# A ConvNeXt-V2 block on one core: where rstd's broadcast stands, which quarters are channel-major, and who normalises one block in ten

## The chip, the core and the metric

The kernel runs on one core of a Trainium2 chip. The metric is the device time of one execution in microseconds, told as the median of several runs. The core's engines are TensorE (PE, with its weight loads shown as PEld), VectorE (DVE), ScalarE (ACT), GpSimd (POOL) and SyncE (SP), which here only issues DMAs.

## The reference

The input x is one image of 512 x 512 pixels with 96 channels, in bf16. E is 384.

```python
out = sum over i, j of xp[:, i:i+H, j:j+W, :] * dw[i, j]      # 3x3 depthwise convolution
h = _layernorm(out, axis=-1)                                  # over the 96 channels
h = gelu(einsum('bhwc,ce->bhwe', h, w1))                      # 96 -> 384
gx = sqrt((h * h).sum(axis=(1, 2), keepdims=True) + 1e-6)     # per channel, over the whole image
nx = gx / (gx.mean(axis=-1, keepdims=True) + 1e-6)
h = grn_gamma * (h * nx) + grn_beta + h
return x + einsum('bhwe,ec->bhwc', h, w2)                     # 384 -> 96
```

The sum of squares over the whole image stands between the two matrix products, so everything up to gelu has to be seen once before the second product can begin.

## The kernel before, in words

The image is cut into 128 blocks of four rows (`NBLK`, `GR`). The kernel has two phases. The first computes the convolution, the normalisation, the first product and gelu of every block, and gathers the sum of squares per channel. The second phase makes gelu again or takes it from where it was kept, multiplies it by the scaled w2, and adds x. The change is in the first phase alone.

The first phase is a software pipeline written out by hand, in slots. In slot s the convolution of block s runs, and the first product of a block some 14 earlier (`mlp`). A table `at`, filled by `put(slot, what, block or batch)`, says which stages belong to a slot, and the loop over s issues them in a fixed order. Every instruction is kept in program order on its engine, so this order is also the queue of each engine, SP's DMA queue included. From the middle of the first phase on, ten slots follow a fixed cycle, since the kinds of blocks repeat with the block's number modulo ten.

The stages that matter here:

- `load_x`, `turn_x`: SP loads the rows of x, and VectorE transposes them into channel-major form (tile xT).
- `conv_taps`: TensorE makes the 3x3 convolution as three bursts of 24 small matmuls (PS<-xT,Wq). `evac` copies the result to y_bf: ScalarE alone (128x1536), or, when the block of the slot's first product has exactly two channel-major quarters (`shared`), ScalarE two thirds and VectorE one third.
- `stage_sq` (GpSimd squares y_bf into ysq), `stage_stats` (TensorE sums over channels, rowsel matmuls), `stage_moments` (VectorE).
- `stage_rstd`, `stage_newton`: GpSimd's small operations that make 1/sqrt(variance) for a batch of four blocks. `stage_turn`: VectorE transposes the result (rt<-rstd). `stage_rows`: SP writes it to DRAM (r_dram<-rt, two DMAs). `stage_bcast`: SP reads it back, spread over partitions (rbc<-r_dram, four DMAs).
- `stage_norm`: GpSimd multiplies y_bf by rbc (yn<-y_bf,rbc). `stage_write` and `stage_read` take yn through DRAM to the layout of the first product (ynT).
- `mlp_units`: the first product of a block, in nine units; each is some matmuls into PSUM followed by one gelu of ScalarE into g. PSUM gives the units one buffer of two banks and two of one bank.

The sum of squares has two ways. A block's 2048 pixels are four quarters. A quarter that is channel-major (`cm_quads` says how many the block has) has its channels on partitions; VectorE reads it with three bn_stats (`entry`, bst<-g). A quarter that is pixel-major has its pixels on partitions; TensorE multiplies it with itself in 128x128 matmuls (gram matmuls, PS<-g), of which the diagonal is used. `grams` is the list of what is owed, two entries for each pixel-major quarter, and each entry is six matmuls. `gram_next(n)` runs the next n entries. In the slot of a block its own entries are added at the end, so they run in later slots. With the convolution running, each slot calls `gram_next(1)` twice.

Blocks whose number modulo ten is in `WHOLE` (0, 3, 7) have four channel-major quarters, and their g is stored to DRAM; the others have two or three. The slot's order of the stages above the product is:

```python
load_x(s + 4); stage_read; stage_write; stage_bcast; stage_rows; store_next()
stage_newton(k, pool); stage_sq; stage_norm; stage_rstd(k, pool)
```

For a batch whose last statistics are made in slot t, rstd is due in t+1, newton and turn in t+2, rows in t+3, the broadcast in t+4, and the first block's norm in t+5.

Of the kernel before, what the change touches and what calls it, by code (L numbers as in the profile page):

```python
# [17 lines left out]
BATCH = 4  # L18
NHELD = 5
WHOLE = (0, 3, 7)  # L20
NTAIL = 14
GRB = 3

# [33 lines left out]
def kernel(  # L57
# [23 lines left out]
    NBLK = H // GR  # L81
# [18 lines left out]
    def cm_quads(q):  # L100
        if is_whole(q) or is_held(q):
            return NQ
        if q > HELD[0]:
            return 1
        return 2 if q >= NBLK - 16 or (q - 1) % 10 in WHOLE else 3

    whole = [q for q in range(NBLK) if is_whole(q)]
    g_dram = dram.tile([len(whole), 128, NQ * NCH * QW], bf16, name="g_dram")
# [78 lines left out]
    with ExitStack() as p1:  # L187
        pe, dve, act, pool, sp = (InOrder(tc, e) for e in (nc.tensor, nc.vector, nc.scalar, nc.gpsimd, nc.sync))
# [324 lines left out]
        def stage_sq(b, on_act):  # L513
            q = ysqpool.tile([128, NI, W], bf16, name="ysq")
            if on_act:
                act.activation(out=q[:], in_=ybf[b][:], func=ACTF.Square)
            else:
                pool.tensor_tensor(out=q[:], in0=ybf[b][:], in1=ybf[b][:], op=ALU.mult)
            ysq[b] = q
# [88 lines left out]
        def stage_turn(k):  # L608
            NT = (BATCHES[k][1] * GR * NG + 31) // 32 * 32
            rt = rtpool.tile([128, NS], bf16, name="rt")  # L610
            dve.transpose(out=rt[:, :NT], in_=rns.pop(k)[:, :NT])
            rts[k] = rt
# [19 lines left out]
        def stage_bcast(k):  # L632
            b0, n = BATCHES[k]
            rbc = rbcpool.tile([128, BATCH, W], bf16, name="rbc")
            for j in range(GR):
                sp.dma_start(out=rbc[32 * j:32 * j + 32, :n, :].rearrange("p n w -> p (n w)"),
                             in_=bass.AP(r_dram[b0].tensor, r_dram[b0].offset + j * n * W, [[0, 32], [1, n * W]]))
            rbcs[k] = rbc
# [39 lines left out]
        def mlp_tail(b, get):  # L678
            if is_held(b) or b < HELD[0]:
                gs[b] = gpool.tile([128, NQ, NCH, QW], bf16, name="g")[:]  # L680
            elif b > NBLK - 4:
                gs[b] = late.gr.tile([128, NQ, NCH, QW], bf16, name="gr")[:]
            else:
                gs[b] = g_over
            for t in range(NQ):
                cm = t < cm_quads(b)
                (cm_unit if cm else px_unit)(gs[b], ynts[b], t)
                gram_next(1)
                if cm:
                    for j in range(NCH):  # L690
                        entry(b, j, t)
                if t == 1:
                    for k in get("turn"):
                        stage_turn(k)
                if t == 2:
                    for b2 in get("stats"):
                        stage_stats(b2)
                if t > cm_quads(b):
                    grams.extend((b, (t - 1) * QC + k * E) for k in range(0, GR, 2))
            for k in get("moments"):  # L700
                stage_moments(k)
            if cm_quads(b) < NQ:
                grams.extend((b, (NQ - 1) * QC + k * E) for k in range(0, GR, 2))
# [49 lines left out]
        def store_next():  # L753
            if stores:
                b, h = stores.pop(0)
                n = NCH * QW * NQ // 3
                sp.dma_start(out=g_dram[whole.index(b)][:, h * n:h * n + n],
                             in_=flat(b)[:, h * n:h * n + n])
# [41 lines left out]
        def put(s, what, v):  # L800
            at.setdefault((s, what), []).append(v)
# [4 lines left out]
        for k, (b0, n) in enumerate(BATCHES):  # L806
            for b in range(b0, b0 + n):
                quick = b not in mlp_slots
                put(b if quick else b + 1, "sqa" if quick else "sqp", b)
                last_s = b + 1 if quick else b + 2  # L810
                put(last_s, "stats", b)
            ramp = b0 + n <= RAMP
            if ramp:
                put(last_s, "chain", k)
                put(last_s + 1, "spread", k)
            else:
                put(last_s, "moments", k)
                put(last_s + 1, "rstd", k)
                put(last_s + 2, "newton", k)
                put(last_s + 2, "turn", k)  # L820
                put(last_s + 3, "rows", k)
                put(last_s + 4, "bcast", k)
            for b in range(b0, b0 + n):
                last_norm = s = max(last_norm + 1, last_s + (1 if ramp else 5))
                put(s, "norma" if ramp else "norm", b)
                put(s + 1, "write", b)
                put(s + 2, "read", b)
                m = s + (3 if ramp else 4)
                mlp_slots.add(m)
                put(m, "mlp", b)  # L830
                put(m + is_whole(b), "combine", b)
                last_slot = m
# [4 lines left out]
        turn_x(2)  # L837
        for s in range(last_slot + 1):
            get = lambda kind: at.get((s, kind), [])
            if s + 4 < NBLK:  # L840
                load_x(s + 4)
            for b in get("read"):
                stage_read(b)
            for b in get("write"):
                stage_write(b)
            for k in get("bcast"):
                stage_bcast(k)
            for k in get("rows"):
                stage_rows(k)
            store_next()  # L850
            for k in get("newton"):
                stage_newton(k, pool)
            for b in get("sqp"):
                stage_sq(b, False)
            for b in get("norm"):
                stage_norm(b)
            for k in get("rstd"):
                stage_rstd(k, pool)
            mlp = get("mlp")

            def spread_out():
                for k in get("spread"):
# [6 lines left out]
            if mlp and mlp[0] >= TAIL0:  # L869
                assert not taps  # L870
                square_owed()
                mlp_tail(mlp[0], get)
            elif not mlp:
                if s + 3 < NBLK:
                    turn_x(s + 3)
                for f in taps:
                    f()
                if not spare:
                    spread_out()
                if evac:  # L880
                    evac()
                for b in get("sqa"):
                    stage_sq(b, True)
                for b in get("stats"):
                    stage_stats(b)
                for k in get("moments"):
                    stage_moments(k)
                if spare:
                    spread_out()
                for k in get("chain"):  # L890
                    stage_moments(k)
                    stage_chain(k)
                for k in get("turn"):
                    stage_turn(k)
                gram_next(2)
                square_owed()
            else:
                b = mlp[0]
                unit, squares, squares_rest = mlp_units(b)
                conv = lambda n, fence=True: taps[n](fence) if taps else None  # L900

                conv(0)
                unit(0, 2)
                unit(2, 1)
                squares(0)
                conv(1, False)
                spread_out()
                if s + 3 < NBLK:
                    turn_x(s + 3)
                unit(3, 1)  # L910
                unit(4, 2)
                squares(1)
                gram_next(1 if taps else 2)
                shared = evac is not None and cm_quads(b) == 2
                unit(6, 1)
                if not shared:
                    squares(2)
                unit(7, 1)
                for k in get("turn"):
                    stage_turn(k)  # L920
                conv(2)
                if evac:
                    evac(shared)
                if shared:
                    squares(2)
                gram_next(1 if taps else 2)
                unit(8, 2)
                unit(10, 1)
                for b2 in get("stats"):
                    stage_stats(b2)  # L930
                unit(11, 1)
                for k in get("moments"):
                    stage_moments(k)
                squares_rest(2)
                square_owed()
                if is_whole(b):
                    owed.append(lambda f=squares_rest: f(3))
                grams.extend((b, c) for c in range(cm_quads(b) * QC, NQ * QC, 2 * E))
                if is_whole(b):
                    stores.extend((b, h) for h in range(3))  # L940
# [130 lines left out]
```

## Time and profile before

| what | value |
|---|---|
| median of 3 runs | 1479.4 us (1470.68 to 1481.37) |
| span of the profiled execution | 1475.6 us; its time with what lies around the span isn't listed |
| PE busy | 1394.1 us, 94% |
| VectorE busy | 1183.4 us, 80% |
| ScalarE busy | 1405.9 us, 95% |
| GpSimd busy | 1300.9 us, 88% |
| bn_stats of g (bst<-g) | 1110 of 672 ns, 673.0 us busy |
| norm on GpSimd (yn<-y_bf,rbc) | 126 of 3111 ns |
| gram matmuls (PS<-g, 128x128) | 1464 |
| DMA | 422.03 MB, mean 286 GB/s |

Busy times are shares of the whole span. The first phase ends near 950 us. A wait is written as engine, tile, line, then what ended it, then microseconds in total, count and longest. In a timeline the columns are start, length, engine, line, operation, output<-inputs, shapes, count, and in brackets the idle time of the engine just before it and what ended that. L35 is the line of the helper that records every instruction, so rows are told apart by their tiles.

### The profile page before, as it was taken

How to read it: one execution, taken by the hardware profiler on the slowest of the kernel's cores; microseconds unless marked ns; L12 is line 12 of the kernel's file. 1: busy time of each engine (PE TensorE's matmuls, PEld its weight loads, DVE VectorE, ACT ScalarE, POOL GpSimd, SP SyncE). 2: the span in 40 equal slices, each digit the busy share in tenths (PEclk: the TensorE clock that was granted, in tenths of full speed). 3: DMA queues.
4: the chain of work that ended last, by engine and by line, in shares of the span. 5: the costliest groups of instructions: out<-in, count | busy, mean ns of one | idle time of the engine just before them, and what ended most of it. 6: DMA issues, size and time to landing. Idle time of an engine off the chain costs nothing.

```text
span 1475.6 us, 54538 instructions
## 1 busy us (share of the span) xinstructions
PE 1394.1 (94%) x23125; PEld 810.0 (55%) x23125; DVE 1183.4 (80%) x2174; ACT 1405.9 (95%) x1595; POOL 1300.9 (88%) x923
## 2 busy tenths in 40 slices
PE   8889899999899999999999998889999999999998
PEld 3434444444444444444444445457777777777776
DVE  8849989999899999999999997965555555555555
ACT  7889999999899999999998999999999999999997
POOL 3469989998899999999999998379999999999998
PEclk9999999999999999999999999999999999999999
DMA  6677778888788888888898876669999999999998
GB/s 180 197 204 231 245 231 275 249 266 240 244 254 268 262 275 239 271 258 272 249 276 247 267 230 200 177 226 366 358 328 383 402 392 392 405 381 406 389 390 315
DMA packets 167913, 422.03 MB, mean 286 GB/s; under 512 B 34326, under 2 KB 84182, under 8 KB 163190
## 3 DMA queue, kind: packets, MB, share of 16 engines
q1 hardware_dynamic: 151428, 314.98, 66.0%
q0 software_dynamic: 14880, 103.43, 18.6%
q8 instruction: 181, 2.97, 0.8%
q14 instruction: 62, 0.51, 0.1%
q10 hardware_dynamic: 1362, 0.15, 0.1%
HBM read 262.16 MB, written 156.22 MB: 284 GB/s over the span
## 4 chain that ended last, share of the span: by engine, by line
POOL 31%; PE 22%; ACT 13%; DVE 12%; DMA 11%; issue 7%; SPq 3%; POOLq 0%; ACTq 0%; DVEq 0%
PE PS L35 22%; POOL xb L328 17%; ACT g L35 8%; DVE bst L35 8%; POOL yn L35 7%; DMA xin<-in_x_dram 3%; ACT y_bf L35 3%; SPq L35 3%; DMA ynT<-yn_dram 3%; POOL xr L283 2%; DMA rbc<-r_dram 2%; DVE xT L35 2%; DMA yn_dram<-yn 2%; POOL ysq L35 1%; POOL var L35 1%
## 5 line engine op out<-in xcount | busy, mean ns | idle before, releaser
L35 ACT ACTIVATE g<-PS 128x512 bf16<-128x512 f32 (+2 forms) x1062 | 730.7, 842 | 26.0 <-PE PS L35 22.4
L35 DVE BATCH_NORM_STATS2 bst<-g 128x6 f32<-128x512 bf16 x1110 | 673.0, 672 | 23.5 <-ACT g L35 23.4
L35 ACT ACTIVATE gr<-PS 128x1536 bf16<-128x1536 f32 x360 | 498.5, 1457 | 14.8 <-PE PS L35 10.0
L35 POOL TENSOR_TENSOR yn<-y_bf,rbc 128x1536 bf16<-128x1536 bf16 x126 | 391.6, 3111 | 84.1 <-DMA rbc<-r_dram 50.5
L35 DVE TENSOR_TENSOR o_sb<-PS,xb 128x384 bf16<-128x384 f32 x512 | 277.7, 556 | 221.3 <-PE PS L35 172.0
L35 PE MATMUL PS<-xT,Wq 64*32 64x511 bf16 (+1 forms) x9198 | 347.6, 388 | 29.2 <-DVE y_bf L35 11.7
L328 POOL TENSOR_TENSOR xb<-xr,B2c 128x1536 f32<-128x1536 bf16 x118 | 368.4, 3136 | 1.5
L35 PE MATMUL PS<-ynT,w1p 128*128 128x512 bf16 x1161 | 332.7, 383 | 24.0 <-ACT g L35 5.8
L35 POOL TENSOR_TENSOR ysq<-y_bf 128x1536 bf16<-128x1536 bf16 x114 | 314.1, 2756 | 11.0 <-ACT y_bf L35 9.6
L35 PE MATMUL PS<-ynT,w1s 128*128 128x512 bf16 x1020 | 275.5, 379 | 0.0
L35 PEld LDWEIGHTS <-gr 128*128 128x128 bf16 x4296 | 212.1, 98 | 61.0 <-issue 3.0
L35 PE MATMUL PS<-W2s,gr 128*128 128x96 bf16 x4224 | 223.4, 206 | 2.0 <-DVE o_sb L35 1.8
L35 PEld LDWEIGHTS <-Wq 64*32 64x32 bf16 x9216 | 111.4, 90 | 201.4 <-issue 159.0
L35 ACT ACTIVATE y_bf<-PS 128x1536 bf16<-128x1536 f32 (+2 forms) x135 | 181.7, 1351 | 15.7 <-PE PS L35 10.6
L35 DVE STREAM_TRANSPOSE xT<-xin 128x576 f32<-128x576 f32 (+1 forms) x256 | 181.4, 748 | 12.8 <-DMA xin<-in_x_dram 10.6
L35 PEld LDWEIGHTS <-w1p 128*128 128x128 bf16 x1161 | 89.8, 98 | 180.3 <-issue 123.3
L35 PEld LDWEIGHTS <-g 128*128 128x128 bf16 (+1 forms) x1707 | 105.5, 98 | 89.1 <-issue 57.0
L35 PE MATMUL PS<-w1p,ynT 128*128 128x256 bf16 (+2 forms) x822 | 125.0, 272 | 8.0 <-ACT xT L35 3.2
L35 PE MATMUL PS<-g 128*128 128x128 bf16 x1464 | 123.1, 221 | 4.1 <-DVE PS L35 4.1
L35 PEld LDWEIGHTS <-w1s 128*128 128x128 bf16 x1020 | 81.9, 98 | 40.5
L35 PEld LDWEIGHTS <-gl 128*128 128x128 bf16 x1680 | 83.1, 98 | 30.0 <-issue 8.9
L35 PE MATMUL PS<-W2s,gl 128*128 128x96 bf16 x1680 | 90.3, 206 | 5.2 <-DVE o_sb L35 4.6
(109 smaller groups left out, 708.4 us busy)
## 6 DMA issues: line engine op xcount, KB each, us to landing
xin<-in_x_dram SPq DMA_DIRECT2D x126, 432.0 KB
g_dram<-g SPq DMA_DIRECT2D x105, 512.0 KB
gl<-g_dram POOLq DMA_DIRECT2D x35, 1536.0 KB, 10.7
yn_dram<-yn SPq DMA_DIRECT2D x512, 96.0 KB
ynT<-yn_dram SPq DMA_DIRECT2D x128, 384.0 KB
out_dram<-o_sb SPq DMA_DIRECT2D x127, 384.0 KB
xr<-in_x_dram POOLq DMA_DIRECT2D x123, 384.0 KB, 6.6
ynT<-yn_dram SPq DMA_DIRECT2D x255, 128.0 KB
```

Of the source, the lines that this page charges most:

```text
L35: r = f(*a, **k)
L283: pq.dma_start(out=xr[:], in_=x[0, r0:r0 + GR].rearrange("r w c -> (r w) c").rearrange("(p g) c -> p g c", g=PXP))
L328: pq.tensor_tensor(out=xb[:], in0=grp[q]["xr"][:], in1=bias[:, None, :].to_broadcast([128, PXP, C]), op=ALU.add)
```

## The change

It has three parts, all in the first phase.

1. The turn of a batch moves from slot t+2 to t+3 and to the head of the slot, in every kind of slot. The broadcast (still in t+4) moves to the head too, ahead of the x load, the read and the write; the rows move behind the g store.
2. `TWOS` replaces the old rule for two channel-major quarters: blocks 1, 4, 5, 8 and 9 modulo ten have two (before: 1, 4 and 8), and only 2 and 6 have three. In a slot with a convolution, all gram entries owed are run in that slot, half of them at the first call and the rest at the second.
3. In a slot whose product is that of a block 5 modulo ten (`DNORM`), the norm due there is done by VectorE, after the product's fifth unit, and not by GpSimd.

```diff
+TWOS = (1, 4, 5, 8, 9)
+DNORM = 5
...
-        return 2 if q >= NBLK - 16 or (q - 1) % 10 in WHOLE else 3
+        return 2 if q >= NBLK - 16 or q % 10 in TWOS else 3
...
-                put(last_s + 2, "turn", k)
+                put(last_s + 3, "turn", k)
...
             get = lambda kind: at.get((s, kind), [])
+            for k in get("turn"):
+                stage_turn(k)
+            for k in get("bcast"):
+                stage_bcast(k)
             if s + 4 < NBLK:
                 load_x(s + 4)
             for b in get("read"):
                 stage_read(b)
             for b in get("write"):
                 stage_write(b)
-            for k in get("bcast"):
-                stage_bcast(k)
+            store_next()
             for k in get("rows"):
                 stage_rows(k)
-            store_next()
...
+            mlp = get("mlp")
             for b in get("norm"):
-                stage_norm(b)
+                if not (s < NBLK and mlp and mlp[0] % 10 == DNORM):
+                    stage_norm(b)
...
                 unit(4, 2)
+                if b % 10 == DNORM and taps:
+                    for b2 in get("norm"):
+                        stage_norm(b2, dve)
                 squares(1)
-                gram_next(1 if taps else 2)
+                gram_next((len(grams) + 1) // 2)
...
                 unit(7, 1)
-                for k in get("turn"):
-                    stage_turn(k)
                 conv(2)
...
-                gram_next(1 if taps else 2)
+                gram_next(len(grams))
```

The two other calls of `stage_turn` (in slots without a product and in the last blocks' routine) go as well.

More of the change, by code (lines that the diff above doesn't have):

```diff
@@ L691, in mlp_tail @@
                         entry(b, j, t)
-                if t == 1:
-                    for k in get("turn"):
-                        stage_turn(k)
                 if t == 2:
@@ L854 @@
                 stage_sq(b, False)
+            mlp = get("mlp")
             for b in get("norm"):
-                stage_norm(b)
+                if not (s < NBLK and mlp and mlp[0] % 10 == DNORM):
+                    stage_norm(b)
             for k in get("rstd"):
                 stage_rstd(k, pool)
-            mlp = get("mlp")
             def spread_out():
@@ L892 @@
                     stage_chain(k)
-                for k in get("turn"):
-                    stage_turn(k)
                 gram_next(2)
@@ L918 @@
                 unit(7, 1)
-                for k in get("turn"):
-                    stage_turn(k)
                 conv(2)
```

## The prediction

> **What bounds the kernel now.** I read the page's busy table first, then windows over the first phase, then the waits, then two short timelines. The table shows four compute engines nearly full:
>
> ```profile
> PE 1394.1 (94%) x23125; PEld 810.0 (55%) x23125; DVE 1183.4 (80%) x2174; ACT 1405.9 (95%) x1595; POOL 1300.9 (88%) x923
> ```
>
> The average hides the phases. The change touches only the first phase (convolution and first matrix product, up to about 950 us). So I cut its regular part into nine stretches of ten slots, one slot for each block's first matrix product (blocks 20 to 109):
>
> ```profile
> core 0: us, PE busy (x) PEld busy (x) DVE busy (x) ACT busy (x) POOL busy (x), PEclk, DMA share, GB/s
> 216.64:286.32 69.68, 67.61 (x1231) 33.12 (x1230) 69.48 (x124) 69.32 (x101) 62.82 (x55) 1.00 0.86 272
> 286.32:357.90 71.58, 68.37 (x1231) 33.39 (x1230) 69.85 (x125) 69.60 (x101) 66.57 (x45) 1.00 0.79 240
> 357.90:433.51 75.61, 69.29 (x1231) 33.66 (x1230) 71.08 (x127) 69.88 (x101) 66.74 (x55) 0.98 0.84 258
> ...
> sum 645.76, PE 617.54 PEld 300.55 DVE 632.38 ACT 627.39 POOL 599.27; mean PE 68.62 PEld 33.39 DVE 70.26 ACT 69.71 POOL 66.59
> ```
>
> The columns after the length are busy microseconds. Ten slots take 71.75 us on average (645.76 / 9). VectorE is busy 70.26 of them, ScalarE 69.71, GpSimd 66.59. The best ten took 69.68 us, with VectorE and ScalarE both full; the worst took 75.61. So there is a floor near 69.7 that VectorE and ScalarE set together, and 71.75 - 69.68 = 2.07 us per ten slots in which somebody waits. The waits of the span and one long stall say who:
>
> ```profile
> POOL yn L35 <- DMA rbc<-r_dram: 50.5, 17, 12.0
> DVE rt L35 <- POOL rstd L35: 17.4, 9, 4.5
> PE PS L35 <- DVE y_bf L35: 11.7, 13, 4.3
> ```
>
> ```profile
> 368.03 3.11 POOL L35 TENSOR_TENSOR yn<-y_bf,rbc 128x1536 bf16<-128x1536 bf16 x1 [3.23 <-DMA xin<-in_x_dram]
> ...
> 375.69 0.25 DVE L35 STREAM_TRANSPOSE rt<-rstd 128x64 bf16<-128x64 bf16 x1 [2.93 <-POOL rstd L35]
> 376.56 1.28 PE L35 MATMUL PS<-xT,Wq 64*32 64x512 bf16 x23 [4.30 <-DVE y_bf L35]
> 378.42 0.60 ACT L35 ACTIVATE g<-PS 128x512 bf16<-128x512 f32 x1 [5.10 <-PE PS L35]
> ```
>
> This is one chain: GpSimd starts its normalisation 3.23 us late (it waited for the broadcast rstd; the releaser named is the queue's neighbour), so its Newton steps are late, so VectorE stands 2.93 us in front of the turn of rstd. Queued behind the turn is VectorE's third of the evacuation (y_bf), so TensorE stands 4.30 us and ScalarE 5.10. GpSimd can't catch up: two long operations a slot plus the rstd chain every fourth slot leave it little.
>
> TensorE's own pace shows in a slot whose block has two channel-major quarters:
>
> ```profile
> 391.97 0.88 PE L35 MATMUL PS<-xT,Wq 64*32 64x512 bf16 x24
> ...
> 393.45 0.50 PE L35 MATMUL PS<-g 128*128 128x128 bf16 x6
> 393.79 0.60 PE L35 MATMUL PS<-w1p,ynT 128*128 128x384 bf16 x4
> ...
> 395.13 0.51 PE L35 MATMUL PS<-g 128*128 128x128 bf16 x6
> 395.47 0.82 PE L35 MATMUL PS<-w1p,ynT 128*128 128x128 bf16 x6
> 396.13 0.45 PE L35 MATMUL PS<-rowsel,y_bf 128*128 128x4 bf16 x12
> ...
> 398.78 0.86 PE L35 MATMUL PS<-xT,Wq 64*32 64x512 bf16 x24
> ```
>
> Starts count here, since ends overlap. From one convolution to the next, 391.97 to 398.78, is 6.81 us with almost no gap: TensorE runs at about 6.8 us a slot. Six gram matmuls (PS<-g) take 0.34 us (393.45 to 393.79), and every slot has two such sets.
>
> **The change, part by part.** By the program's order it has 66 fewer bn_stats of g, 22 more VectorE casts of y_bf, 264 more gram matmuls, and 11 normalisations on VectorE instead of GpSimd. Per ten slots that is two more blocks with two quarters and one VectorE normalisation.
>
> VectorE: 6 bn_stats go, at 0.60 us from start to start (seven in 4.23 us in the row at 376.43): -3.6. Two casts come, at 0.58 (375.85 to 376.43): +1.2. One normalisation comes; its only VectorE rows are the ramp's two, 0.938 us each: +0.9. Sum -1.5, so 70.26 becomes 68.8.
>
> ScalarE: twice the evacuation shrinks from 128x1536 to 128x1024. From start to start that is 1.34 against 0.90 us (388.65 to 389.99; 395.60 to 396.50): -0.9, so 68.8.
>
> GpSimd: one normalisation of 3.11 us less: 66.59 becomes 63.5. It gets room to recover after a late transfer.
>
> TensorE: four more gram sets at 0.34 us: +1.4. The third quarter itself costs the same either way: six pixel-major matmuls take 0.66 us (395.47 to 396.13), three 128x512 at 0.22 take 0.65.
>
> That +1.4 is unevenly spread. Before, two sets ran in each slot. Now everything owed by the block before runs at once: none after a whole block, two sets after one with three quarters, four after one with two, half of them in the middle and half after the convolution. Slots 0 to 9 of a ten get 4, 0, 4, 2, 0, 4, 4, 2, 0, 4 sets. I take a slot as the larger of TensorE's and ScalarE's need, because the product has only a two-bank and two one-bank buffers between them:
> - no set (1, 4, 8): TensorE 6.81 - 0.68 = 6.13; ScalarE 6.98 (a three-quarter slot, 405.71 to 412.69) - 0.44 = 6.54. Takes 6.55.
> - two sets (3, 7, both whole blocks): as now, 7.03.
> - four sets (0, 2, 5, 6, 9): 6.81 + 0.68 = 7.49. Slots 2, 5 and 9 follow a slot with none, in which TensorE can run about 0.15 ahead (an estimate from when the buffers come free): 7.33. For 0 and 6 I take 7.45.
>
> Sum: 3 x 6.55 + 2 x 7.03 + 3 x 7.33 + 2 x 7.45 = 70.6 us per ten slots. It lies above VectorE's 68.8 and GpSimd's 63.5, so both have slack and I let the waits of 2.07 go: 71.75 - 70.6 = 1.15 us gained per ten slots. The bounds: 68.8 per ten if buffers smooth the bursts wholly; 71.9 if light slots stay at the 6.83 that two-quarter slots take now and each heavy one costs 7.4 to 7.6.
>
> The turn: it leaves the middle of one slot for the head of the next, some 3 us later, and so waits less for Newton. Queued behind it on VectorE are the slot's bn_stats and the cast. Late next would be the rows' DMAs: they were issued at 414.39, the turn was at 406.21, so 8 us of cover become 5. Price 0; without that cover, up to 3 us a batch.
>
> The broadcast: it now stands directly behind the rows on SP (before, 5.7 us apart: 414.39 and 420.05), so SP waits for the rows to land. No row shows that landing. It is at least the 0.6 us of an issue and at most the 4.86 us of a 96 KB yn_dram transfer in the chain of waits; I take 2. Behind it stand an x load (four slots ahead), a ynT read (two slots ahead of its use), four yn writes (three buffers) and a g store. SP's issues in four slots come to about 20 of 28 us, so 0 is charged; if that slack were gone, 3 us per batch. The broadcast itself lands 2 to 3 us sooner. rstd's own operations are the same.
>
> VectorE's normalisation can't meet a late broadcast: it takes blocks 9, 19, 29 and so on, never the first of a batch of four.
>
> In all, blocks 5 to 113 make 10.9 tens: 10.9 x 1.15 = 12.5 us. The second phase isn't touched. The profiled span is 1475.6 us (what lies around it isn't listed); the median is 1479.4, the runs 1470.68 to 1481.37, so the span is an ordinary one. 1475.6 - 12.5 = 1463.1; on the median, 1467.
>
> **Rivals.**
> *The bursts are absorbed.* VectorE and ScalarE at 68.8, with small waits, give at best the 69.68 already seen or a little less: 2.1 to 2.9 us per ten, 23 to 32 in all, so 1447 to 1456. For it: PEld's column is only 47% of the stretch. Against it: two-quarter slots already run at TensorE's pace of 6.81, with no gap to fill.
> [...]
>
> *Nothing moves.* The waits are fed by transfers that stay late (the read and write of yn through DRAM), and the bursts eat what the lighter VectorE gives: 1479.
>
> *Slower: TensorE becomes the bound in half the slots.* Light slots stay at 6.83 and heavy ones cost 7.4 to 7.6, so ten slots take 71.9 without any wait; with 1.2 us of the present 2.07 still lost they take 73.1: 10.9 x 1.4 = 15 us more, 1494. It decides once what is won in the light slots and on waits is under 1.3 us per ten. For it: five of ten slots are above 7 us by TensorE alone. Against it: ScalarE's 0.44 us are real in every light slot.
>
> *The turn waits all the same.* If GpSimd stays late by a slot, the turn at the slot's head stands where it stood. VectorE stood 7.7 us in front of it between 200 and 880 us, some 0.8 per ten slots, which leaves 0.35 of the 1.15: 4 us, 1475.
>
> **How the numbers follow.** Forecast 0.50 (own range 1457 to 1477), absorbed 0.20, nothing moves or the turn still waits 0.15, slower 0.15. A measurement tells about 1% from no change, 14.8 us: 1464.6 and 1494.2. Faster: all of the absorbed case and 0.18 of the forecast, 0.38. Slower: some 0.12, from the slower case, whose middle lies at that bound and whose upper part reaches 1505. Same: 0.50. The range 1448 to 1492 leaves out the best end of the absorbed case and the upper half of the slower one.
>
> **What would show it.** Right: ten-slot stretches of 70 to 71 us, with no DVE wait for rstd and no POOL wait for rbc over 1 us; slots with four sets 7.3 to 7.5 us, those with none 6.5 to 6.6; ScalarE idle in the heavy slots behind PE PS. Wrong: heavy slots at 7.0 (absorbed), light ones at 6.8 (slower), or stalls of 3 us and more that stay; a VectorE wait for rbc; SP's loads of x late.

## The result, and the profile after

The changed kernel takes 1486.82 us (median of 16 runs, 1477.79 to 1493.42) against 1477.5 for the kernel before (16 runs beside them, 1470.68 to 1484.99). The ratio is 1.0056, 95% interval [1.0037, 1.0074]: some 8 us slower, where the forecast was 12.5 faster. The profiled execution took 1479.93 (span 1478.1); it is one of the fastest of its kernel, so its trace holds less of the loss than an ordinary run. That matters below.

The busy row of the page after:

```profile
PE 1407.7 (95%) x23455; PEld 827.9 (56%) x23455; DVE 1170.4 (79%) x2137; ACT 1398.9 (95%) x1595; POOL 1266.4 (86%) x912
```

VectorE, ScalarE and GpSimd have less to do than before, TensorE more, as planned, and the time still rises. The nine stretches of ten slots (blocks 20 to 109), in the columns that were used for the kernel before (two of them and the sum):

```profile
...
434.75:505.74 70.99, 69.15 (x1261) 34.81 (x1260) 69.09 (x122) 68.93 (x101) 63.42 (x45) 1.00 0.83 253
505.74:579.49 73.75, 70.29 (x1261) 35.11 (x1260) 67.44 (x120) 69.49 (x101) 63.50 (x55) 1.00 0.80 248
...
sum 643.79, PE 625.64 PEld 313.99 DVE 621.19 ACT 622.06 POOL 573.70; mean PE 69.52 PEld 34.89 DVE 69.02 ACT 69.12 POOL 63.74
```

No stretch is under 70.99, and the mean is 643.79 / 9 = 71.53. VectorE at 69.02, ScalarE at 69.12 and GpSimd at 63.74 all have slack on average; three of the nine stretches take 71.0, with nothing late in them. That is TensorE's bursts. A slot with four gram sets, by TensorE's timeline:

```profile
256.08 0.87 PE L37 MATMUL PS<-xT,Wq 64*32 64x512 bf16 x24
256.88 0.86 PE L37 MATMUL PS<-ynT,w1p 128*128 128x512 bf16 x3
257.58 0.83 PE L37 MATMUL PS<-g 128*128 128x128 bf16 x12
...
259.59 0.84 PE L37 MATMUL PS<-g 128*128 128x128 bf16 x12
260.27 0.82 PE L37 MATMUL PS<-w1p,ynT 128*128 128x128 bf16 x6
...
263.57 1.16 PE L37 MATMUL PS<-xT,Wq 64*32 64x512 bf16 x24
```

Each pair of sets now stands together (x12, 0.67 and 0.68 us to the next start), and from convolution to convolution it is 263.57 - 256.08 = 7.49 us.

The waits inside the stretches (216 to 865 us), first in the kernel before:

```profile
POOL yn L35 <- DMA rbc<-r_dram: 13.6, 11, 2.1
PE PS L35 <- DVE y_bf L35: 10.3, 10, 4.3
DVE rt L35 <- POOL rstd L35: 7.7, 5, 2.9
```

and in the changed one:

```profile
DVE xT L37 <- DMA xin<-in_x_dram: 4.9, 3, 2.1
PE PS L37 <- DVE y_bf L37: 1.8, 4, 0.7
POOL yn L37 <- DMA rbc<-r_dram: 1.6, 1, 1.6
```

GpSimd's wait for rbc has fallen, TensorE's for y_bf too, and VectorE's for rstd is gone. What has grown is VectorE's wait in front of the turn of x (2.2 us in two stands before): its loads land late. The two long stands of the three are what made the worst stretch, 505.74 to 579.49. For the first of them, in SyncE's queue:

```profile
526.28 1.84 SPq L37 DMA_DIRECT2D r_dram<-rt  x2
530.54 2.11 SPq L37 DMA_DIRECT2D rbc<-r_dram  x4
532.70 0.42 SPq L37 DMA_DIRECT2D xin<-in_x_dram  x1
```

and on VectorE and TensorE a few microseconds on:

```profile
538.60 1.44 DVE L37 STREAM_TRANSPOSE xT<-xin 128x576 f32<-128x576 f32 x2 [2.01 <-DMA xin<-in_x_dram]
...
541.13 0.67 DVE L37 CAST y_bf<-PS 128x512 bf16<-128x512 f32 x1
...
541.85 0.86 PE L37 MATMUL PS<-xT,Wq 64*32 64x512 bf16 x23 [0.63 <-DVE y_bf L37]
```

SyncE holds the broadcast until the rows have landed (rows issued at 526.28, broadcast at 530.54), then issues its four DMAs, and only then the x load, at 532.70. VectorE wants that load in the next slot, stands 2.01 us, and gets it at 538.6, 5.9 us after its issue. Behind the turn its share of the evacuation is late, and TensorE waits for it. In all of the stretches SyncE's queue waited for the rows (total, count, longest):

```profile
SPq L37 <- DMA r_dram<-rt: 33.0, 22, 2.4
```

### The profile page after: what moved, and what is told of

Its sections match the earlier page's. It is cut to its first block, busy times and chain, and to the rows that moved or that the text cites. A ratio compares the mean times of both kernels' runs of the same rounds, so it can differ in the third digit from the quotient of the medians.

```text
span 1478.1 us, 55169 instructions
## 1 busy us (share of the span) xinstructions
PE 1407.7 (95%) x23455; PEld 827.9 (56%) x23455; DVE 1170.4 (79%) x2137; ACT 1398.9 (95%) x1595; POOL 1266.4 (86%) x912
## 4 chain that ended last, share of the span: by engine, by line
PE 27%; POOL 26%; ACT 18%; DMA 10%; DVE 9%; issue 5%; SPq 4%; ACTq 0%; POOLq 0%; DVEq 0%
PE PS L37 27%; POOL xb L330 21%; ACT g L37 13%; DMA yn_dram<-yn 7%; DVE bst L37 5%; SPq L37 4%; ACT y_bf L37 3%; POOL xr L285 3%; DVE xT L37 2%; DMA r_dram<-rt 1%; ACT xT L37 1%; ACT gr L37 1%; DMA xin<-in_x_dram 1%; POOL yn L37 1%; POOL gl L296 1%
## 5 line engine op out<-in xcount | busy, mean ns | idle before, releaser
L37 DVE BATCH_NORM_STATS2 bst<-g 128x6 f32<-128x512 bf16 x1044 | 639.3, 674 | 49.9 <-ACT g L37 49.2
L37 POOL TENSOR_TENSOR yn<-y_bf,rbc 128x1536 bf16<-128x1536 bf16 x115 | 356.8, 3105 | 52.4 <-ACT rbc L37 25.2
L37 PE MATMUL PS<-xT,Wq 64*32 64x511 bf16 (+1 forms) x9198 | 342.2, 388 | 15.5 <-ACT y_bf L37 4.1
L37 PE MATMUL PS<-ynT,w1p 128*128 128x512 bf16 x1095 | 310.4, 382 | 26.8 <-ACT g L37 5.6
L37 PEld LDWEIGHTS <-w1p 128*128 128x128 bf16 x1095 | 84.2, 97 | 183.0 <-issue 119.1
L37 ACT ACTIVATE y_bf<-PS 128x1024 bf16<-128x1024 f32 (+2 forms) x135 | 169.4, 1260 | 16.2 <-PE PS L37 10.6
L37 PE MATMUL PS<-w1p,ynT 128*128 128x384 bf16 (+1 forms) x954 | 148.8, 273 | 12.0 <-ACT xT L37 3.2
L37 PEld LDWEIGHTS <-g 128*128 128x128 bf16 (+1 forms) x1971 | 117.3, 98 | 64.1 <-issue 39.1
L37 PEld LDWEIGHTS <-ynT 128*128 128x128 bf16 x954 | 74.6, 97 | 62.2 <-issue 39.2
```

Source lines behind the costliest of these rows:

```text
L37: r = f(*a, **k)
```

## The experiments

Each ratio is to the kernel before, run on the same chip beside it (its medians there lay between 1472.3 and 1477.5), so ratios are compared and not medians. "Order", "quarters" and "norm" are parts 1, 2 and 3 of the change.

| run | order | quarters | norm on VectorE | further edit | median us | ratio, 95% |
|---|---|---|---|---|---|---|
| changed kernel | yes | yes | yes | | 1486.82 | 1.0056 [1.0037, 1.0074] |
| p1_order | yes | | | | 1473.38 | 1.0009 [0.9992, 1.0026] |
| p2_quarters | | yes | | | 1481.12 | 1.0067 [1.0043, 1.0092] |
| p3_dnorm | | | yes | | 1502.07 | 1.0205 [1.0185, 1.0225] |
| p23 | | yes | yes | | 1489.7 | 1.0124 [1.0101, 1.0146] |
| p12 | yes | yes | | | 1487.34 | 1.0079 [1.0048, 1.0110] |
| before_again | | | | | 1475.77 | 1.0001 [0.9983, 1.0019] |
| smooth | yes | yes | yes | gram sets spread | 1482.53 | 1.0046 [1.0023, 1.0069] |
| xfirst | yes | yes | yes | x load first | 1478.35 | 1.0001 [0.9976, 1.0025] |
| xfirst_gpnorm | yes | yes | | x load first | 1479.1 | 1.0005 [0.9983, 1.0027] |
| smooth_xfirst | yes | yes | yes | both | 1469.8 | 0.9953 [0.9928, 0.9978] |
| smooth_xfirst_gpnorm | yes | yes | | both | 1468.07 | 0.9953 [0.9934, 0.9973] |
| p1_xfirst | yes | | | x load first | 1464.36 | 0.9931 [0.9905, 0.9958] |
| p2_spread | | yes | | gram sets spread | 1475.08 | 0.9992 [0.9962, 1.0022] |
| best | yes | yes | | both, late sums | 1465.61 | 0.9921 [0.9895, 0.9947] |

Not in the table: p3_oneinput, and three more runs on the end of the first phase.

### One part at a time

The three edits are those of the change. p1_order:

```diff
-                put(last_s + 2, "turn", k)
+                put(last_s + 3, "turn", k)
...
+            for k in get("turn"):
+                stage_turn(k)
+            for k in get("bcast"):
+                stage_bcast(k)
             if s + 4 < NBLK:
                 load_x(s + 4)
...
```

> The kernel before with the first part alone: turn at the head of its slot a slot later, broadcast first, rows last. Theory Q (queue): the broadcast ahead of the x load makes SP stand some 1.5 us for the rows to land and then issue four DMAs, so x loads come late; the first part alone costs time: 1480 to 1490 against 1477.5 before, with VectorE waits of about 2 us for x in xT. Theory B (bursts): the first part only removes the waits for rstd and rbc, some 0.8 us per ten slots or more: 1465 to 1471.

p2_quarters:

```diff
-        return 2 if q >= NBLK - 16 or (q - 1) % 10 in WHOLE else 3
+        return 2 if q >= NBLK - 16 or q % 10 in TWOS else 3
...
-                gram_next(1 if taps else 2)
+                gram_next((len(grams) + 1) // 2)
...
-                gram_next(1 if taps else 2)
+                gram_next(len(grams))
```

> The kernel before with the second part alone: two quarters in five blocks of ten, all gram entries owed run in the next slot. Both theories expect heavy slots of 7.4 to 7.5 us and light ones of 6.55 to 6.65, a sum of 71.0 us per ten without waits. Theory B: waits for rstd and rbc stay, since GpSimd is as tight as before: 72 to 73 per ten, 1481 to 1491. Theory Q: VectorE's 1.5 us less let the waits shrink, 71 to 71.4 per ten: 1468 to 1474.

p3_dnorm:

```diff
             for b in get("norm"):
-                stage_norm(b)
+                if not (s < NBLK and mlp and mlp[0] % 10 == DNORM):
+                    stage_norm(b)
...
+                if b % 10 == DNORM and taps:
+                    for b2 in get("norm"):
+                        stage_norm(b2, dve)
```

> The kernel before with the third part alone: VectorE normalises one block in ten. Both theories: GpSimd has 3.1 us per ten slots to recover in and the waits for rstd shrink, but VectorE, busy 70.26 of 71.75 us per ten, gets 0.94 more and becomes the bound at 71.2 per ten: 1470 to 1476. If VectorE's busy time were no bound, 70 per ten: 1459.

p23, the changed kernel without its first part:

> The changed kernel without its first part (order of turn, broadcast and rows as before). Theory Q: without late x loads the ten slots come to the 71.0 us of their slots: 1468 to 1476, so 10 to 18 us faster than the changed kernel's 1486.8. Theory B: the bursts are the cost and the order helps: 1486 to 1492.

No theory held throughout. p1_order came out between the two. p2_quarters has theory B's time and theory Q's ten slots (71.07 us). p23, with the old order, was as slow as theory B said, so late x is not the whole loss. p3_dnorm missed both.

The order alone is worth nothing that can be measured, although the waits that it was to remove have shrunk (for rbc 4.2 us) or gone (for rstd). The quarters alone, with their bursts, cost 0.67%. The norm alone costs 2.05%, some 30 us, and that was not foreseen at all. Some 7 of them lie at the end of the first phase, which is looked at below; the mechanism of the rest is in the trace of p3_dnorm:

```profile
333.63 2.75 POOL L36 TENSOR_TENSOR ysq<-y_bf 128x1536 bf16<-128x1536 bf16 x1 [0.72 <-ACT y_bf L36]
333.80 3.39 DVE L36 TENSOR_TENSOR yn<-y_bf,rbc 128x1536 bf16<-128x1536 bf16 x1
337.11 2.46 DVE L36 BATCH_NORM_STATS2 bst<-g 128x6 f32<-128x512 bf16 x4
...
340.08 0.49 PE L36 MATMUL PS<-g 128*128 128x128 bf16 x6 [3.14 <-DVE PS L36]
...
340.83 0.60 ACT L36 ACTIVATE g<-PS 128x512 bf16<-128x512 f32 x1 [2.63 <-PE PS L36]
```

VectorE's product starts 0.17 us after GpSimd's square and ends 0.81 us after the square does: it did its own work only when GpSimd had finished. What is queued behind it on VectorE is late, so TensorE stands 3.14 us and ScalarE 2.63. The spread of the same operation in p3_dnorm, and then in the changed kernel (ns, least, median, most):

```profile
L36 DVE TENSOR_TENSOR yn<-y_bf,rbc x9: 921/3281/3458, 261.8 to 845.5; 128x1536 bf16<-128x1536 bf16 x9
```

```profile
L37 DVE TENSOR_TENSOR yn<-y_bf,rbc x9: 914/919/1300, 261.1 to 833.6; 128x1536 bf16<-128x1536 bf16 x9
```

With the other parts in, the two rarely meet, and the norm takes its 0.92. The Trainium skill's "SBUF — State Buffer", section "SBUF: two separate sides", describes such a lock: VectorE and GpSimd share a pair of ports, which goes for the whole instruction to whichever starts first, a GpSimd operation or a VectorE operation with two SBUF inputs or in a two-port mode, and the other engine stands. The trace agrees with it: 3.39 us beside a square of 2.75, against 0.92 with GpSimd quiet. It agrees the other way round too: at 700.38 us VectorE was first and took 0.92, and the square that GpSimd began 0.47 us later took 3.07. The prediction did not reckon with it.

### Bursts or VectorE's norm

before_again is the kernel before, unchanged, for a second profile.

> The kernel before, unchanged, for a second profile of it. If its first profile was an ordinary one, ten slots take 71.5 to 72 us again with stalls of 5 us behind the turn; if that profile was a slow one, ten slots take about 71.0. Ratio 0.998 to 1.002 either way.

Its ten slots took 71.14 us on average where the first profile had 71.75: one profile's waits are no constant of the kernel.

smooth is the changed kernel with its sets spread over the slots as 3,2,2,2,2,3,3,2,2,3 instead of 4,0,4,2,0,4,4,2,0,4:

```diff
-                gram_next((len(grams) + 1) // 2)
+                due = 3 if taps and b % 10 in (0, 5, 6, 9) else 2 if taps else len(grams)
+                gram_next((due + 1) // 2)
...
-                gram_next(len(grams))
+                gram_next(due // 2)
```

> The changed kernel with the same 24 gram entries per ten slots spread as 3, 2, 2, 2, 2, 3, 3, 2, 2, 3 instead of 4, 0, 4, 2, 0, 4, 4, 2, 0, 4. Theory B (bursts): slots with three entries 7.15 us, with two 6.8 to 7.0, in all 70.0 per ten instead of 71.0, so 10 to 11 us faster than the changed kernel, ratio to before 0.998. Theory L (the loss is VectorE's normalisation and the end of the phase, where VectorE's two-input operations stand while GpSimd works): no more than 3 us faster than the changed kernel, ratio 1.003 to 1.006.

p12 is the changed kernel with all normalisations on GpSimd (its third part undone).

> The changed kernel without its third part (GpSimd normalises every block). Theory L: 4 to 8 us faster than the changed kernel, ratio 1.000 to 1.003. Theory B: GpSimd's 3.1 us come back and with them waits for rstd and rbc: as slow as the changed kernel or slower, 1.006 to 1.009.

Neither settled it. By its ratio smooth fits theory L and p12 theory B, and the two contradict each other. The time hardly moved in either, and both profiles suggest why: x was late more often in them. The wait in p12 (216 to 865 us), which had 3 occurrences in the changed kernel's profile:

```profile
DVE xT L36 <- DMA xin<-in_x_dram: 27.5, 16, 3.2
```

In smooth it was 21.4 us in 18 waits. The next runs therefore took late x away.

p3_oneinput is p3_dnorm with another operation, and asked whether a VectorE operation with one SBUF input escapes GpSimd. It multiplies y_bf by 1 through strided views, so the product with rstd is left out.

```diff
+            if one:
+                eng.tensor_scalar(out=yn[:].rearrange("p i w -> p w i"), in0=ybf.pop(b)[:].rearrange("p i w -> p w i"),
+                                  scalar1=1.0, scalar2=None, op0=ALU.mult)
...
-                        stage_norm(b2, dve)
+                        stage_norm(b2, dve, True)
```

> The kernel before with the third part, but VectorE's operation in the block's place reads only y_bf, in a strided order, and leaves out the product with rstd. Theory L (a VectorE operation with two SBUF inputs waits for GpSimd's running operation): the operation takes the same 1.6 us or so every time, whatever GpSimd does, slots 6 and 8 lose their 4 us stalls, ratio to before 1.000 to 1.008 instead of 1.0205. Rival (VectorE is simply full, or waits for a transfer): the duration still spreads up to 3 us and the ratio stays at 1.018 or above.

1526.1 us, 1.0345 [1.0316, 1.0373]: a miss. The operation took 4.19 to 6.46 us, not 1.6, and stretched GpSimd's squares from 2.75 to as much as 6.65. Where it began ahead of the square, it took 4.2 (at 417.38: 4.19, and the square that began 0.08 later 6.61); where it began well inside one, 5.7 to 6.5. So 4.2 us is its own length, and again whoever came second stood. This form doesn't escape; whether one with unit strides would, the run doesn't tell.

### Late x

xfirst moves one line of the changed kernel:

```diff
             for k in get("turn"):
                 stage_turn(k)
-            for k in get("bcast"):
-                stage_bcast(k)
             if s + 4 < NBLK:
                 load_x(s + 4)
+            for k in get("bcast"):
+                stage_bcast(k)
```

> The changed kernel with one edit: the x load stands ahead of the broadcast on SyncE again (turn, x load, broadcast, read, write). Nothing else differs. Theory L (late x): in the changed kernel VectorE stood 16.0 us for xin between 220 and 870 us, in eight stands, because the wait for the rows to land sits ahead of an x load that is used one slot later. Without it xT's stands fall under 3 us, and slots 5 to 9 lose their outliers (8.49, 8.57, 7.95): ten-slot stretches 70.9 to 71.1 instead of 71.53, the time 5 to 9 us shorter, 1478 to 1482 if the changed kernel's is 1486.8. Theory B (bursts alone): the stands fill time that the heavy slots' TensorE would take anyway, so ten slots stay at 71.5 and the time at 1485 to 1488. A third way: the broadcast, now a little later, makes GpSimd wait for rbc again, by the 0.8 us of an x load's issue at most, under 2 us in all.

smooth_xfirst makes both edits, smooth_xfirst_gpnorm keeps the norm on GpSimd besides:

> The changed kernel with two edits: the x load ahead of the broadcast, and the gram entries spread as 3,2,2,2,2,3,3,2,2,3 over the ten slots instead of 4,0,4,2,0,4,4,2,0,4. Theory L plus B: the spread alone had a floor of 70.0 us per ten slots (four slots of 7.13, four light of 6.81, the whole ones of 7.0) but lost 2.1 in each ten to late x (21.4 us of xT stands). With x on time ten slots take 70.0 to 70.4, 1.1 to 1.5 less than the changed kernel's 71.53: the time is 12 to 17 us under the changed kernel's, 1470 to 1475, and xT's stands are under 3 us. If late x is not what keeps the spread version at 72.1, its ten slots stay at 71.5 or more and the time at 1480 or more.

> As the run before, but the norm of blocks 9, 19, 29 stays on GpSimd. What is tested is the worth of the third part where nothing else is late. Theory N (it costs, as VectorE can be shut out by GpSimd): the version without it is 2 to 5 us faster. Theory W (it pays: GpSimd has 66.6 of 70.2 us busy without it, 63.5 with it, so after a late transfer it catches up): the version without it is 4 to 10 us slower, with POOL waits and VectorE waits for rstd in it. No difference, within 2 us, if GpSimd has enough room either way and the VectorE row takes its 0.92 us.

One figure in xfirst's expectation is misread: 16.0 us in eight stands is VectorE's wait for xin in the whole span. Between 216 and 865 us it is the 4.9 in three that were shown above, in a run that was among the fastest. The x load ahead of the broadcast takes the whole loss away (1.0056 to 1.0001), and no wait for xin is left in xfirst's stretches (71.19 us per ten slots, a little above the 71.1 expected, in a run above its kernel's median); theory L held. The same exchange of one line was worth 0.74% between p12 and xfirst_gpnorm, 0.78% between p1_order and p1_xfirst and 0.93% between smooth and smooth_xfirst, so it doesn't hang on one pair. The third way fell: GpSimd's norm (yn) had no wait for rbc. Spreading the sets, which had given 0.1% with late x, gives 0.5% without it. smooth_xfirst's profile is of its slowest run (1483.55, 70.75 us per ten slots, above the 70.4 expected): slot 6, the one after VectorE's norm, takes 7.9 us there with VectorE busy for all but 0.04 of it, and 7.07 in smooth_xfirst_gpnorm. In the medians the norm on VectorE makes no difference (0.9953 both), so neither theory on its worth held, and the third outcome named did; its runs only spread wider (1463.75 to 1483.55 against 1466.49 to 1472.78).

xfirst_gpnorm asks the same with the bursts kept:

> The changed kernel with the x load ahead of the broadcast and without its third part: all normalisations on GpSimd, the gram bursts kept. Against the run with the third part (1478.35). Theory N (VectorE's row meets GpSimd and VectorE is full in slots 5 and 6): 2 to 4 us faster, 1474 to 1476. Theory W (GpSimd's spare time lets it catch up): 4 us or more slower, 1482 and over. No difference if it stays within 2 us, as with the spread entries (1469.8 against 1468.07).

1.0005 against 1.0001: none either. Its ten slots took 71.06 us on average, those of smooth_xfirst_gpnorm 70.11. The two differ only in how the gram sets are spread, so bursts cost 0.95 us per ten slots, 10.4 us over the 10.9 tens; the ratios differ by 0.0052, 7.7 us.

Two last runs price the parts without the disturbance. p1_xfirst is the order alone with the x load first, p2_spread the quarters alone with the sets spread (the edits above):

> The kernel before with the new order alone, and the x load ahead of the broadcast. The order alone was 1.0009 [0.9992, 1.0026] of the kernel before, with 70.63 us per ten slots in a profile that was its fastest run (1467.53). Theory L (late x gives back what the order saves): now 1465 to 1469, a ratio of 0.992 to 0.995. If the waits for rbc and rstd were in the shade of something else, the ratio stays at 0.999 to 1.002, 1474 to 1478.

> The kernel before with the second part alone, but with the gram entries spread 3,2,2,2,2,3,3,2,2,3. With the bursts it was 1.0067 [1.0043, 1.0092]. Theory B (the bursts cost, the quarters do not): 0.4 to 1.0 us per ten slots less, and the ratio between 0.998 and 1.003. If the quarters cost by themselves (264 more gram sets on TensorE), it stays at 1.005 to 1.008.

Both ratios are as expected: the order is worth 0.7% when x isn't late, and the quarters cost nothing when the sets are spread. The stretches expected of p2_spread were not seen: 71.54 us per ten slots against 71.07 in p2_quarters. But the one profile is of a run above its kernel's median (1480.36), the other of one below (1476.54). In the first VectorE stood 16.2 us for rstd, in the second 1.6. The cleaner pair is the one without waits above. The stretches of p1_xfirst:

```profile
215.42:285.17 69.75, 67.53 (x1231) 33.12 (x1230) 69.55 (x124) 69.32 (x102) 66.30 (x56) 1.00 0.89 272
...
777.61:848.21 70.60, 68.50 (x1231) 33.40 (x1230) 70.30 (x126) 69.69 (x102) 67.57 (x57) 1.00 0.86 265
sum 632.79, PE 613.63 PEld 299.70 DVE 630.55 ACT 626.63 POOL 601.29; mean PE 68.18 PEld 33.30 DVE 70.06 ACT 69.63 POOL 66.81
```

632.79 / 9 = 70.31 us per ten slots, with VectorE busy 70.06 of them: this is the floor of the old quarters, without waits. And its runs lie between 1463.77 and 1464.82, where those of the kernel before spread over 16 us in the same session. That suggests that the spread is made of these waits; no run shows it by itself.

### The end of the first phase

From block 110's first product to the first o_sb the profiles show 112 to 122 us, 113.0 in the changed kernel and 120.8 in p23 and in p3_dnorm. There VectorE's sums over the moments meet GpSimd's first three xb. In p23, and then in the changed kernel:

```profile
959.20 2.27 DVE L37 TENSOR_TENSOR parts<-mom 128x66 f32<-128x66 f32 x1
961.51 6.16 DVE L37 TENSOR_TENSOR parts<-parts,mom 128x66 f32<-128x66 f32 x2
```

```profile
958.72 0.23 DVE L37 TENSOR_TENSOR parts<-mom 128x66 f32<-128x66 f32 x1
958.99 0.53 DVE L37 TENSOR_TENSOR parts<-parts,mom 128x66 f32<-128x66 f32 x2
```

Three small operations take 8.43 us instead of 0.76 when GpSimd is at work. An operation with one input can stand as well: in xfirst's profile the TENSOR_SCALAR that follows (parts<-parts, 128x66 f32) took 3.03 us beside xb, against 0.20 in the changed kernel. The edit that puts them off:

```diff
                     load_xr(n, sp)
-                second_moments(0, NACC - 1)
...
-        second_moments(NACC - 1, NACC)
+        second_moments(0, NACC)
```

> Parts two and three without part one (1489.7 us, its profile's stretch from block 110's product to the first o_sb 120.8 us) with one edit: VectorE's sums over the moments (parts, 128x66) are done after the loop, when GpSimd's first three xb are over. Theory C (collision): two parts of 0.27 us alone took 3.06 us each, and one 2.27, beside xb, and the last squares stood behind them. Then parts take 0.2 to 0.3 each, the stretch falls to 114 to 116 us and the time by 4 to 7 us, to 1483 to 1486. If the tail was long for another reason (VectorE behind with its moments), the stretch stays at 119 to 122 and the time near 1490.

> The changed kernel with VectorE's sums over the moments (parts) done after the loop, so that they can't meet GpSimd's first three xb. Theory C: the meeting, some 7 us when it is met in full and chance from run to run, is in most runs of the changed kernel; its profiled run (1479.93, the stretch from block 110's product to the first o_sb 113.0) had none. Then the time falls to 1480 to 1483, and the lowest runs stay near 1478. Theory L (late x alone makes the 9 us): the time stays at 1485 to 1488 and the spread as it was (1478 to 1493).

> The kernel before with the same edit. Theory C: its two profiles had stretches of 112.3 and 114.8 us, so it meets little; 1474 to 1477, within 3 us of the kernel before, and the changed kernel gains more from the edit than this one. If the collision is as common here as after the change, both gain the same 4 to 7 us, and it says nothing of the difference between them.

p23_late fell to 1.0054 [1.0033, 1.0075] from 1.0124, its stretch from 120.8 to 113.0. after_late is at 1.0051 [1.0030, 1.0073] and before_late at 1.0001 [0.9982, 1.0019], no different from the kernels that they come from (after_late's 1483.77 us lies between the two theories' ranges). So the meeting is real and cost p23 its tail, but no part of the changed kernel's loss is shown to come from it: theory C fell. The edit isn't a full cure either; in after_late the first of the sums still met the last xb and took 2.65 us. The meeting was also in the profiles of xfirst (118.8 us) and xfirst_gpnorm (121.7). Neither was run with the sums put off, so their ratios may hold some of it, and late x may cost more than the exchange of the line shows.

### Both findings together

best has the order with the x load first, the quarters with spread sets, all norms on GpSimd and the sums put off.

> The order of the changed kernel with the x load ahead of the broadcast, two quarters in five of ten blocks with the gram entries spread 3,2,2,2,2,3,3,2,2,3, all normalisations on GpSimd, and the sums over the moments after the loop. Without the last edit this was 1468.07. The stretch at the end was 115.8 us there with one part of 3.04 us in it, so 113 and 1464 to 1467 are expected; more if that meeting is commoner than the profile shows. Ten-slot stretches stay at 70.1.

1465.61 us, 0.9921 [0.9895, 0.9947]; ten slots take 69.92 us. The stretch at the end was not the 113 expected but 117.0: the first of the sums still met the last xb (2.98 us). best is faster than both kernels. p1_xfirst, which has the order alone, is as fast within the intervals: its ten slots take 0.39 us more, some 4 us over the 10.9 tens, but its end takes 113.4. So parts two and three of the change have not been shown to gain anything in any combination.

## Why the prediction was wrong, point by point

Between 12.5 us forecast as a gain and 8 measured as a loss lie some 20 us. Two steps failed: the x load behind the broadcast, priced at 0, accounts for some 8 of them, and the gain of 1.15 us per ten slots, which wasn't there, for the rest.

- **First failed step: the x load behind the broadcast, priced at 0.** The prediction put "an x load (four slots ahead)" there. `load_x(s + 4)` is four blocks ahead of the convolution, but the next reader of the load is `turn_x(s + 3)`, in the slot after: it has one slot of cover, and 5.9 of some 7 us passed from issue to turn. The wait for the rows itself was near its estimate (33.0 us in 22 waits, 1.5 each, where "I take 2"). The price of the delay was 0.55% of the time, 8 us (xfirst against the changed kernel). The argument that SyncE had slack ("some 20 of 28 us") answered another question: not whether its queue keeps up, but how late one transfer may go out.
- **Second failed step: the gain of 1.15, 71.75 less 70.6.** 70.6 was a floor without waits, and 71.75 a mean with them, from one profile (71.14 in the second). Floor against floor, the kernel before has 70.31 (p1_xfirst), not the 69.68 of its best ten, and the changed one 71.0: the bursts are a loss of 0.7 us per ten slots, which the prediction's sum counted as part of a gain. Alone they cost 0.67%.
- **"Both have slack and I let the waits of 2.07 go."** Right about the cause: with x on time the order alone gains 0.7%. That is 10 us, less than half of the 22.6 that 2.07 per ten slots would be over 10.9 tens. The gain and the bursts' loss cancel (xfirst, at 1.0001, has both), and late x comes on top. p1_order, without the bursts, is at 1.0009. There it is the exchanged line that shows what late x took; its one profile is of its fastest run, with a single stand of 1.9 us.
- **The bursts.** From one block's first gelu to the next's (medians of nine), light slots took 6.55 to 6.64, nearly as forecast, and whole ones 6.93 and 6.99 (7.03 forecast). Slots 2, 5 and 9 took 7.5, so the lead that made them 7.33 isn't there; no run shows it. Slot 0 took 7.40 and slot 6 7.72 (7.41 where GpSimd makes all norms, in xfirst_gpnorm; both forecast at 7.45). The sum without late x is 71.0, not 70.6.
- **VectorE's normalisation at 0.938.** Right in the changed kernel by luck of the timing (median 0.919), wrong as a price: beside GpSimd's work it is 3.3, and the ramp's two rows came from a time when GpSimd was quiet. Even at 0.92 it isn't free: it leaves VectorE next to no idle time in slot 6, which takes 7.57 us on average in xfirst and 7.41 in xfirst_gpnorm. That is too little to be seen in the medians. Why the quarters move the norm away from GpSimd's squares wasn't tried.
- **Engine loads.** VectorE 69.02, ScalarE 69.12 and GpSimd 63.74 per ten slots, against 68.8, 68.8 and 63.5. GpSimd's room bought nothing (xfirst_gpnorm).
- **The rivals.** "Slower" named TensorE's bursts as its mechanism and the light slots at 6.83 as its place. The heavy slots did cost the 7.4 to 7.6 that it named, but the light ones did not stay at 6.83, and the bursts by themselves only cancel what the order gains with x on time. VectorE's wait for rstd is gone, so "the turn waits all the same" fell. The absorbed case leaned on the weight-load share, by which half of TensorE's time was free. But spreading the same sets, with the share hardly changed (34.9 us of ten slots in the changed kernel, 34.5 in best, which has them spread), gave 0.5%: the start-to-start rows were the better guide.
- Among the signs of a wrong forecast, "SP's loads of x late" is the one that showed.

## What to carry to other kernels

When a DMA that has to wait is moved ahead in a queue, look up for every transfer behind it when its next reader starts, not how many blocks ahead its data are: here one line, the x load ahead of the broadcast, decided between 8 us lost and none. Compare a floor only with a floor: a burst of work that fits the engine on average still costs in the slots that it fills, and the waits of one profile can hide that. And before work goes from GpSimd to VectorE, see what GpSimd does at that moment.

## What the hardware showed that was not expected

- In these traces VectorE's operation with two SBUF inputs stands until GpSimd's running operation has ended: 0.92 us alone, 3.39 beside a square of 2.75, and two sums over 66 columns 6.16 together instead of 0.53. A one-input f32 operation did so too (3.03 instead of 0.20), and where VectorE began first, GpSimd's square stood (3.07 and up to 6.65 instead of 2.75). The profile books the stand as busy time, so it can't be found among the waits, only in the durations.
- With x on time the order alone ran within 1.05 us from least to most over its runs, the kernel before over 16.2.
